# Token-group transposes of a normalized activation by DMA instead of the matmul engine, with group 0's hidden layer moved ahead of its queries

## Chip, cores and metric

The kernel runs on one core of one Trainium2 chip. The metric is the device time in microseconds (us) of one execution; medians of several executions are quoted. Engines are named as in the profile: PE is the matmul engine, PEld its weight loads, DVE the vector engine, ACT the scalar engine, POOL the general one, SP the one that issues the DMA transfers.

Ratios are the mean time of one kernel's fast runs over the mean of the other's fast runs in the same rounds, so they are not quite the ratio of the medians quoted beside them. "Fast" is the state without a disturbance that every run is labelled with.

## The reference

One block for 2048 tokens of width D = 640, all in bf16: `xn` is the layer norm of x, and the result is x plus a linear attention of `xn` plus a feed-forward of `xn`.

```python
def reference(A_x, A_wqkv, A_wo, B_x, B_w1, B_b1, B_w2, B_b2):
    x = A_x
    xn = _layernorm(x)                       # (x - mean) / sqrt(var + 1e-5)
    q, k, v = split(xn @ A_wqkv)             # 32 heads of 20
    pq, pk = phi(q), phi(k)                  # phi(t) = where(t > 0, t + 1, exp(t)) + 1e-6
    kv, z = sum_s pk v^T, sum_s pk           # per head
    attention = (pq kv) / (pq z + 1e-6) @ A_wo
    feed_forward = gelu(xn @ B_w1 + B_b1) @ B_w2 + B_b2      # hidden width 1536
    return x + attention + feed_forward
```
(Shortened: the reshapes are left out.)

## The kernel before

The 2048 tokens are 16 tiles of 128, in 4 groups of 512. `xn` has the tokens on the partitions. The matmuls need the model dimension there, so every tile of `xn` is also transposed into `xnT`: five 128x128 blocks, each a PE matmul against the identity, then one copy from the accumulator bank to `xnT`.

```python
def emit_T(t, copy, c0=0, c1=NC):            # NC = 5
    n = c1 - c0
    pT = bank(BF16)[:, 0 : n * P].rearrange("p (c n) -> p c n", c=n)
    for c in range(n):
        nc.tensor.transpose(pT[:, c, :], xn[:, t, (c0 + c) * P : (c0 + c + 1) * P], identity[:])
    copy(out=xnT[:, c0:c1, t * P : (t + 1) * P], in_=pT)
```

Each group runs K (4 tiles), Q (5 blocks of 5 matmuls), and h (the hidden layer, 12 blocks of 5 matmuls). While a group's h runs on PE, DVE prepares the next group (statistics, 1/sqrt by Newton steps, normalization), and the transposes of the next group are put between the last blocks of h.

```python
for g in range(NG):
    t0, t1 = g * TPG, (g + 1) * TPG
    if g > 0:
        for i in range(TPG):
            emit_K(t0 + i)
    for m in range(NC):
        emit_Q(g, m)
    for j in range(NJ):                       # NJ = 12
        emit_h(g, j)
        # ... cut: sums of pk, masks, late work of the last group ...
        if g == NG - 1:
            continue
        if j < TPG:
            emit_stats(t1 + j)
        if j == TPG:
            emit_rstd_vector(t1, t1 + TPG)    # 13 small DVE operations
        if TPG <= j < 2 * TPG:
            emit_norm(t1 + j - TPG)
        if j > 2 * TPG:
            emit_T(t1 + j - 2 * TPG - 1, nc.scalar.copy)
        if j == NJ - 1:
            emit_T(t1 + TPG - 1, nc.scalar.copy)
```

All loads are issued from SP at the start, in this order: x of tiles 0 and 1, K weights, x of tiles 2 and 3, K weights, Q weights, x of group 1, w1, b1, x of groups 2 and 3, b2, wv, wo, w2.

## Time and profile before

| | before |
|---|---|
| time, median | 213.5 us (213.2 to 214.2, 16 runs) |
| span of the profiled run | 211.9 us |
| PE busy | 98% |
| DVE, ACT busy | 53%, 39% |
| share of PE in the chain that ended last | 95% |

The chain is the work that decided the end: it is followed back from the last instruction, at each step to what released it. These are lines of the profile's page for the kernel before: the span, the busy time of each engine (share of the span, number of instructions), and, from the part on the chain that ended last, the shares of the engines.

```profile
span 211.9 us, 3417 instructions
PE 207.4 (98%) x1393; PEld 119.8 (57%) x1393; DVE 112.2 (53%) x265; ACT 82.8 (39%) x134; POOL 13.3 (6%) x41
...
PE 95%; DMA 3%; SPq 1%; DVE 0%; issue 0%
```

The page is to be read together: PE is nearly always busy, and the chain of work that decides the end is PE's own queue. Shortening work of DVE or ACT buys nothing here. Taking an instruction away from PE buys its time, as long as nothing makes PE wait instead.

What five transposes cost is seen in the chain in order of time, here around the end of group 0's h and the start of group 1's K (start in us, length in us, what, number of instructions). L377 is h, L253 the transposes, L285 is K.

```profile
27.93 2.37 PE bank L377 x11
30.30 0.28 PE bank L253 x5
30.59 1.08 PE bank L377 x5
31.66 0.28 PE bank L253 x5
31.94 1.08 PE bank L377 x5
33.02 0.56 PE bank L253 x10
33.58 1.08 PE bank L285 x5
```

Four sets of five take 1.12 us per group. The groups of instructions say something else for the same matmuls (busy time, then mean ns of one, then idle time before them):

```profile
L253 PE MATMUL bank<-identity,xn 128*128 128x128 bf16 x70 | 5.7, 219 | 0.0
L254 ACT COPY xnT<-bank 128x640 bf16<-128x640 bf16 x13 | 8.6, 690 | 0.5 <-PE bank L253 0.5
```

A single transpose is on record with 219 ns, but the records of a set overlap: five of them take 0.28 us of the chain, 56 ns each. The chain is the view to cost a PE instruction from.

### The profile page before, as it was taken

The page shows a single profiled execution, that of the slowest core. Times are in us where ns is not written, and L with a number is a line of the kernel's source. Part 1 is how long each engine was busy: PE and PEld are TensorE (multiplying, and loading weights), DVE is VectorE, ACT ScalarE, POOL GpSimd, SP SyncE. Part 2 cuts the span into 40 slices and gives each one's busy share as a digit, 9 for nine tenths or more (in the row PEclk, how much of TensorE's full clock was granted, in tenths as well). Part 3 has the DMA queues.
Part 4 walks back from the last instruction along what each step waited for, and adds up shares of the span by engine and source line. Part 5 has one row for each costly group of instructions (what it writes and reads, how often), then busy time and mean ns, then how long its engine had stood idle before and what let it go on. Part 6 is the DMA issues. An engine that isn't in the chain of part 4 may idle for free.

```text
span 211.9 us, 3417 instructions
## 1 busy us (share of the span) xinstructions
PE 207.4 (98%) x1393; PEld 119.8 (57%) x1393; DVE 112.2 (53%) x265; ACT 82.8 (39%) x134; POOL 13.3 (6%) x41
## 2 busy tenths in 40 slices
PE   8999999999999999999999999999999999999993
PEld 2454455544554445544445657677777777777752
DVE  3779950998969995698980021773221121121111
ACT  3576769686786868767441221220000000000000
POOL 1000000000000007000019500000000000000000
PEclk9999999999999999999999999999999999999998
DMA  6999970000000000000049968001101100000111
GB/s 200 348 382 331 361 270 1 5 0 0 0 3 0 0 2 3 0 0 0 3 91 200 195 202 318 10 0 62 34 31 51 45 31 31 31 34 31 59 37 31
DMA packets 13278, 18.17 MB, mean 86 GB/s; under 512 B 2432, under 2 KB 11344, under 8 KB 13264
## 3 DMA queue, kind: packets, MB, share of 16 engines
q1 hardware_dynamic: 13264, 17.97, 27.1%
q8 instruction: 11, 0.18, 0.4%
q14 instruction: 3, 0.02, 0.0%
HBM read 12.72 MB, written 5.24 MB: 85 GB/s over the span
## 4 chain that ended last, share of the span: by engine, by line
PE 95%; DMA 3%; SPq 1%; DVE 0%; issue 0%
PE bank L553 25%; PE bank L377 25%; PE bank L561 10%; PE bank L368 10%; PE bank L470 8%; PE bank L285 8%; DMA wqk<-in_A_wqkv_dram 3%; PE bank L479 2%; PE bank L295 2%; PE bank L253 2%; PE bank L521 1%; PE bank L572 1%; PE bank L339 1%; SPq L127 0%; PE bank L576 0%; PE bank L531 0%
## 5 line engine op out<-in xcount | busy, mean ns | idle before, releaser
L553 PE MATMUL bank<-w,hT 128*128 128x320 bf16 (+2 forms) x384 | 57.3, 299 | 0.0
L377 PE MATMUL bank<-xnT,w 128*128 128x512 bf16 x240 | 53.8, 379 | 0.0
L553 PEld LDWEIGHTS <-hT 128*128 128x128 bf16 x384 | 36.9, 98 | 15.6 <-issue 0.5
L565 DVE TENSOR_TENSOR late<-bank,x_all 128x320 bf16<-128x320 f32 (+2 forms) x32 | 15.7, 492 | 52.2 <-PE bank L561 52.2
L377 PEld LDWEIGHTS <-w 128*128 128x128 bf16 x240 | 23.1, 98 | 26.9 <-issue 0.4
L381 ACT ACTIVATE hT<-bank,b1col 128x512 bf16<-128x512 f32 x48 | 32.6, 687 | 14.0 <-PE bank L377 13.2
L269 ACT ACTIVATE e<-bank 128x512 bf16<-128x512 f32 x40 | 23.0, 596 | 11.7 <-PE bank L368 7.1
L561 PE MATMUL bank<-late,pqT 128*128 128x320 bf16 (+2 forms) x160 | 26.5, 299 | 0.0
L368 PE MATMUL bank<-xnT,wqk 128*128 128x512 bf16 x100 | 22.2, 379 | 0.0
L285 PE MATMUL bank<-wqk,xnT 128*128 128x512 bf16 x80 | 20.4, 379 | 0.1
L561 PEld LDWEIGHTS <-pqT 128*128 128x128 bf16 x160 | 15.5, 98 | 6.3
L270 DVE TENSOR_SCALAR e<-e 128x512 bf16<-128x512 bf16 x40 | 11.4, 285 | 13.6 <-ACT e L269 13.6
L470 PE MATMUL bank<-pk,xn 128*128 128x512 bf16 x80 | 18.1, 379 | 0.0
L368 PEld LDWEIGHTS <-wqk 128*128 128x128 bf16 x100 | 9.6, 98 | 10.9
L206 DVE BATCH_NORM_STATS2 stats<-x_all 128x6 f32<-128x320 bf16 x32 | 13.7, 466 | 3.3 <-DMA x_all<-in_A_x_dram 3.3
L273 DVE SCALAR_TENSOR_TENSOR pk<-bank,e 128x512 bf16<-128x512 f32 x20 | 13.8, 692 | 1.0
L273 DVE SCALAR_TENSOR_TENSOR pqT<-bank,e 128x512 bf16<-128x512 f32 x20 | 13.8, 692 | 0.7
L489 DVE TENSOR_TENSOR pqT<-pqT,xnT 128x2048 bf16<-128x2048 bf16 x5 | 6.0, 1215 | 15.4 <-DMA xnT<-rec_rows 15.4
L470 PEld LDWEIGHTS <-xn 128*128 128x128 bf16 x80 | 7.7, 98 | 8.5
L359 DVE TENSOR_TENSOR zacc<-zacc,pk 128x640 f32<-128x640 f32 x13 | 10.8, 829 | 0.4
L285 PEld LDWEIGHTS <-xnT 128*128 128x128 bf16 x80 | 7.1, 98 | 5.6 <-issue 0.4
L471 ACT CAST GT<-bank 128x512 bf16<-128x512 f32 x5 | 2.9, 587 | 16.9 <-PE bank L470 16.9
(68 smaller groups left out, 124.6 us busy)
## 6 DMA issues: line engine op xcount, KB each, us to landing
w<-in_B_w_dram SPq DMA_DIRECT2D x2, 1920.0 KB, 10.0
rec_rows<-recT SPq DMA_DIRECT2D x4, 640.0 KB, 8.3
xnT<-rec_rows SPq DMA_DIRECT2D x5, 512.0 KB, 6.7
out_dram<-late SPq DMA_DIRECT2D x15, 160.0 KB, 1.8
x_all<-in_A_x_dram SPq DMA_DIRECT2D x3, 640.0 KB, 9.3
wqk<-in_A_wqkv_dram SPq DMA_DIRECT2D x1, 800.0 KB
wv<-in_A_wqkv_dram SPq DMA_DIRECT2D x1, 800.0 KB
woA<-in_A_wo_dram SPq DMA_DIRECT2D x5, 160.0 KB, 7.5
```

The source lines that it names most:

```text
L206: nc.vector.bn_stats(out=st[:, half, :], in_=x_all[:, t, half * HALF : (half + 1) * HALF])
L269: nc.scalar.activation(out=e[:], in_=ps[:], func=ACT.Exp)
L270: nc.vector.tensor_scalar(out=e[:], in0=e[:], scalar1=1.0, scalar2=1e-6, op0=ALU.min, op1=ALU.add)
L273: nc.vector.scalar_tensor_tensor(out=dst, in0=shaped(ps), scalar=0.0, in1=shaped(e), op0=ALU.max, op1=ALU.add)
L285: nc.tensor.matmul(K_ps[t][:], lhsT=xnT[:, k, t * P : (t + 1) * P], rhs=wqk[:, k, D : D + TOK], start=(k == 0), stop=(k == NC - 1),)
L368: nc.tensor.matmul(ps[:], lhsT=wqk[:, k, m * P : (m + 1) * P], rhs=xnT[:, k, gs], start=(k == 0), stop=(k == NC - 1),)
L377: nc.tensor.matmul(ps[:], lhsT=w1[:, k, j * P : (j + 1) * P], rhs=xnT[:, k, g * TOK : (g + 1) * TOK], start=(k == 0), stop=(k == NC - 1),)
L381: nc.scalar.activation(out=hT[g][:, j, :], in_=ps[:], func=ACT.Gelu_apprx_tanh, bias=b1col[:, j : j + 1], scale=1.0)
L470: nc.tensor.matmul(ps[:], lhsT=w, rhs=pk[:, t, 0:TOK], start=(t == 0), stop=(t == NT - 1))
L553: nc.tensor.matmul(ps, lhsT=hT[g][:, j, i * P : (i + 1) * P], rhs=w2[:, j, ns], start=(j == 0), stop=False)
L561: nc.tensor.matmul(ps, lhsT=pqT[:, c, t * P : (t + 1) * P], rhs=KVW[:, c, ns], start=False, stop=(c == NC - 1),)
L565: nc.vector.tensor_tensor(out=osb[:, ns], in0=ps, in1=x_all[:, t, ns], op=ALU.add)
```

## The change

Its intent: groups 1 to 3 are transposed by the DMA engines. A group's `xn` is stored to a DRAM buffer, and five transposing DMA transfers (512 rows by 128 columns each) bring it back as `xnT`. That path has a long latency, so the rest of the change makes room for it: group 0's h moves ahead of its Q, w1 is loaded before the Q weights, 1/sqrt goes to POOL, and the loads that are needed late are issued only after group 2's transposes.

```diff
+    def emit_T_dma(g):
+        rows = xn_rows[g]
+        nc.sync.dma_start(
+            out=rows[:].rearrange("(i p) d -> p i d", p=P), in_=xn[:, g * TPG : (g + 1) * TPG, :]
+        )
+        for c in range(NC):
+            nc.sync.dma_start(
+                out=xnT[:, c, g * TOK : (g + 1) * TOK], in_=rows[:, c * P : (c + 1) * P], transpose=True
+            )
 ...
-    def emit_rstd_vector(t0, t1):             # 13 Newton operations on DVE
+    def emit_rstd_pool(t0, t1):
+        r = rstd[:, t0:t1]
+        nc.gpsimd.tensor_scalar(out=r, in0=mv[:, t0:t1, 1], scalar1=EPS, scalar2=None, op0=ALU.add)
+        nc.gpsimd.tensor_tensor(out=r, in0=r, in1=neg_half[:, 0 : t1 - t0], op=ALU.pow)
 ...
     load_wk(3, NC)
+    load_x(4, 8)
+    # b1, then w1 in two halves
     # Q weights
-    # x of group 1, w1, b1
     load_x(8, 12)
-    load_x(12, 16)                            # and b2, wv, wo, w2
+    def load_late(): ...                      # the same five loads
 ...
+    # group 0's K; statistics, rstd and norms of group 1
+    emit_T_dma(1)
+    for t in range(2, TPG + 1):
+        emit_K0phi(t)                         # the rest of group 0's phi(K)
+    # statistics, rstd and norms of group 2
+    emit_T_dma(2)
+    load_late()
     for g in range(NG):
+        if g == 0:
+            for j in range(NJ):
+                emit_h(g, j)
         # K if g > 0, Q, then h if g > 0
+            if g == 1 and j == 0:
+                # statistics, rstd and norms of group 3
+                emit_T_dma(3)
-            if j > 2 * TPG:
-                emit_T(t1 + j - 2 * TPG - 1, nc.scalar.copy)
-            if j == NJ - 1:
-                emit_T(t1 + TPG - 1, nc.scalar.copy)
```
(One of the sums of pk on DVE also moves to the next group's h, and the other sums of groups 1 and 2 and the masks on POOL are issued earlier within it; a fourth buffer for exp is added, and group 0's K banks are held longer.)

More of the change, by code (lines that the diff above doesn't have):

```diff
@@ L12 @@
 F32 = mybir.dt.float32
-I32 = mybir.dt.int32
 @with_exitstack
@@ L70 @@
     small = ctx.enter_context(tc.tile_pool(name="small", bufs=4))
-    etmp = ctx.enter_context(tc.tile_pool(name="etmp", bufs=3))
+    etmp = ctx.enter_context(tc.tile_pool(name="etmp", bufs=4))
     psum = ctx.enter_context(tc.tile_pool(name="psum", bufs=1, space=bass.MemoryType.PSUM))
@@ L82 @@
     rec_rows = dram.tile([H * DH, S], BF16, name="rec_rows")
+    xn_rows = {g: dram.tile([TOK, D], BF16, name=f"xn_rows{g}") for g in range(1, NG)}
     zsum = GT[:, NC - 1, :]
@@ L98 @@
     Z3t = consts.tile([P, NC, H], BF16, name="Z3t")
-    newton = consts.tile([P, 2, TPG], F32, name="newton")
+    neg_half = consts.tile([P, TPG], F32, name="neg_half")
     eps_t = consts.tile([P, 1], F32, name="eps_t")
@@ L135, with load_late @@
     load_wk(3, NC)
+    load_x(4, 8)
+    nc.sync.dma_start(out=b1_bf[:], in_=B_b1.rearrange("(j p) -> p j", p=P))
+    nc.sync.dma_start(out=w1[:, :, 0 : F // 2], in_=w1_v[:, :, 0 : F // 2])
+    nc.sync.dma_start(out=w1[:, :, F // 2 : F], in_=w1_v[:, :, F // 2 : F])
     nc.sync.dma_start(out=wqk[:, :, 0:D], in_=wqkv_v[:, :, 0:D])
-    load_x(4, 8)
-    nc.sync.dma_start(out=w1[:], in_=w1_v)
-    nc.sync.dma_start(out=b1_bf[:], in_=B_b1.rearrange("(j p) -> p j", p=P))
     load_x(8, 12)
-    load_x(12, 16)
-    nc.sync.dma_start(out=b2b[:], in_=B_b2.unsqueeze(0).to_broadcast((P, D)))
-    nc.sync.dma_start(out=wv[:], in_=wqkv_v[:, :, 2 * D : 3 * D])
-    for m in range(NC):
-        nc.sync.dma_start(out=woA[:, m, :], in_=A_wo[e_lo[m] : e_lo[m] + P, :])
-    nc.sync.dma_start(out=w2[:], in_=w2_v)
+    def load_late():
+        load_x(12, 16)
+        nc.sync.dma_start(out=b2b[:], in_=B_b2.unsqueeze(0).to_broadcast((P, D)))
+        nc.sync.dma_start(out=wv[:], in_=wqkv_v[:, :, 2 * D : 3 * D])
+        for m in range(NC):
+            nc.sync.dma_start(out=woA[:, m, :], in_=A_wo[e_lo[m] : e_lo[m] + P, :])
+        nc.sync.dma_start(out=w2[:], in_=w2_v)
     nc.vector.memset(warm, 0.0)
     nc.vector.memset(eps_t[:], EPS)
+    nc.vector.memset(neg_half[:], -0.5)
     make_identity(nc, identity)
@@ L217, in emit_rstd @@
         nc.scalar.activation(out=r, in_=r, func=ACT.Exp, scale=-0.5)
-    def emit_rstd_vector(t0, t1):
-        n = t1 - t0
-        y = rstd[:, t0:t1]
-        v, a = newton[:, 0, 0:n], newton[:, 1, 0:n]
-        nc.vector.tensor_scalar(out=v, in0=mv[:, t0:t1, 1], scalar1=EPS, scalar2=None, op0=ALU.add)
-        nc.vector.tensor_scalar(
-            out=a.bitcast(I32), in0=v.bitcast(I32), scalar1=1, scalar2=None,
-            op0=ALU.logical_shift_right,
-        )
-        nc.vector.tensor_scalar(
-            out=y.bitcast(I32), in0=a.bitcast(I32), scalar1=-1.0, scalar2=float(0x5F3759DF),
-            op0=ALU.mult, op1=ALU.add,
-        )
-        nc.vector.tensor_scalar(out=v, in0=v, scalar1=-0.5, scalar2=None, op0=ALU.mult)
-        for _ in range(3):
-            nc.vector.tensor_tensor(out=a, in0=v, in1=y, op=ALU.mult)
-            nc.vector.tensor_tensor(out=a, in0=a, in1=y, op=ALU.mult)
-            nc.vector.scalar_tensor_tensor(
-                out=y, in0=a, scalar=1.5, in1=y, op0=ALU.add, op1=ALU.mult
-            )
+    def emit_rstd_pool(t0, t1):
+        r = rstd[:, t0:t1]
+        nc.gpsimd.tensor_scalar(out=r, in0=mv[:, t0:t1, 1], scalar1=EPS, scalar2=None, op0=ALU.add)
+        nc.gpsimd.tensor_tensor(out=r, in0=r, in1=neg_half[:, 0 : t1 - t0], op=ALU.pow)
     def emit_norm(t, c0=0, c1=NC):
@@ L265, in emit_T_first, with phi_exp, phi_rest @@
             nc.scalar.copy(out=xnT[:, c0:c1, t * P : (t + 1) * P], in_=pT)
-    def phi(dst, ps, shaped):
+    def phi_exp(ps):
         e = etmp.tile([P, TOK], BF16, name="e")
         nc.scalar.activation(out=e[:], in_=ps[:], func=ACT.Exp)
+        return e
+    def phi_rest(dst, ps, e, shaped):
         nc.vector.tensor_scalar(
@@ L275, in phi @@
         )
+    def phi(dst, ps, shaped):
+        phi_rest(dst, ps, phi_exp(ps), shaped)
     rest_ps = {}
@@ L282, in emit_Ka @@
         if k0 == 0:
-            K_ps[t] = bank()
+            K_ps[t] = bank(hold=t < TPG)
         for k in range(k0, k1):
@@ L408, with emit_K0phi @@
     emit_norm(3)
+    e_of = {}
+    def emit_K0phi(t):
+        if t < TPG:
+            phi_rest(pk[:, t, 0:TOK], K_ps.pop(t), e_of[t], lambda a: a[:])
+        else:
+            phi_rest(
+                pk[:, 0:TPG, TOK:D], rest_ps[0], e_of[t],
+                lambda a: a[:].rearrange("p (t n) -> p t n", t=TPG),
+            )
     emit_Ka(1, 2, NC)
     emit_Kb(1)
-    emit_Kphi(0)
+    e_of[0] = phi_exp(K_ps[0])
+    emit_K0phi(0)
     emit_Ka(2, 0, 2)
@@ L415 @@
     emit_Kb(2)
-    emit_Kphi(1)
-    emit_Kphi(2)
-    emit_K(3)
+    e_of[1] = phi_exp(K_ps[1])
+    e_of[2] = phi_exp(K_ps[2])
+    emit_Ka(3)
+    emit_Kb(3)
+    e_of[3] = phi_exp(K_ps[3])
+    e_of[TPG] = phi_exp(rest_ps[0])
+    emit_stats(4)
+    nc.vector.tensor_copy(out=b1col[:], in_=b1_bf[:])
+    for t in range(5, 8):
+        emit_stats(t)
+    emit_rstd_pool(4, 8)
+    emit_K0phi(1)
+    for t in range(4, 8):
+        emit_norm(t)
+    emit_T_dma(1)
+    for t in range(2, TPG + 1):
+        emit_K0phi(t)
+    for t in range(8, 12):
+        emit_stats(t)
+    emit_rstd_pool(8, 12)
+    for t in range(8, 12):
+        emit_norm(t)
+    emit_T_dma(2)
+    load_late()
     for g in range(NG):
         t0, t1 = g * TPG, (g + 1) * TPG
+        if g == 0:
+            for j in range(NJ):
+                emit_h(g, j)
+                if j == 7:
+                    release()
+            nc.scalar.preload_act_table_set("natural_log_exp_and_others")
         if g > 0:
-            nc.scalar.preload_act_table_set("natural_log_exp_and_others")
+            if g > 1:
+                nc.scalar.preload_act_table_set("natural_log_exp_and_others")
             for i in range(TPG):
@@ L426 @@
             emit_Q(g, m)
-            if g == 0 and m == 2:
-                nc.vector.tensor_copy(out=b1col[:], in_=b1_bf[:])
         if g == NG - 1:
             hT.append(early.tile([P, NJ, TOK], BF16, name="hT3", tag="early"))
-        for j in range(NJ):
+        for j in range(NJ if g > 0 else 0):
             emit_h(g, j)
-            if g == 1 and j == 2 * TPG:
+            if g == 1 and j == 0:
+                for t in range(3 * TPG, NT):
+                    emit_stats(t)
+                emit_rstd_pool(3 * TPG, NT)
+                for t in range(3 * TPG, NT):
+                    emit_norm(t)
+                emit_T_dma(3)
                 emit_zacc(0)
+            if g == 2 and j == 0:
+                gate(hT[g][:, 0, 0:1])
+                emit_masks()
                 emit_zacc(1)
-            if g == 2 and j == 2 * TPG:
-                gate(xn[:, NT - 1, 0:1])
-                emit_masks()
                 emit_zacc(2)
@@ L449 @@
                     emit_xb(t)
-            if g == NG - 1:
-                continue
-            if j < TPG:
-                emit_stats(t1 + j)
-            if j == TPG:
-                emit_rstd_vector(t1, t1 + TPG)
-            if TPG <= j < 2 * TPG:
-                emit_norm(t1 + j - TPG)
-            if j > 2 * TPG:
-                emit_T(t1 + j - 2 * TPG - 1, nc.scalar.copy)
-            if j == NJ - 1:
-                emit_T(t1 + TPG - 1, nc.scalar.copy)
     grest = [None]
```

## The prediction

> **What bounds the kernel now.** The profile's page has the matmul engine (PE) busy 98% of a 211.9 us span; the chain of waits that ended last is 95% PE; the granted clock is 0.997. So a change pays only by taking instructions off PE, and costs only by making PE wait. DVE (53%) and ACT (39%) have room.
>
> **What the change removes from PE.** 12 of the 14 five-fold transposes of line 253 (60 small matmuls). In the chain in order of time, hidden-layer blocks start at 30.59 and 31.94 us with 1.08 us of matmul: 0.27 us per five transposes. The chain gives line 253 1.9%, 4.0 us for 14 sets, which agrees. 12 x 0.275 = 3.3 us, all critical. Also gone: 12 ACT copies of 0.69 us and 39 DVE Newton steps of 0.16 us, off the critical path, worth nothing directly.
>
> **What it adds.** Per group one store of xn to DRAM and five DMA transposes 512x128, plus two small POOL operations. To hide their latency, group 0's hidden layer goes ahead of its Q, and w1 is loaded before the Q weights.
>
> **Does PE have to wait?**
> (a) w1. K of group 0 ends at 14.0 us; then w1's first half is needed. Ahead of it are 2.13 MB, the 2-byte-element load of b1, and its own 0.98 MB. By the GB/s of 1 us windows, 3.1 MB had moved at 11.1 us before; b1 shows as a dip at 15 to 17 us worth 0.9 us; landing trails by about 1.5 us (wqk at 8.4). Estimate: 13.5 us, nearly no margin. I allow 0.3 us.
> (b) The first Gelu waits for five exponentials and a table load (1.28 us) and ends near 16.9 us; three free banks carry PE to 17.3. Fits.
> (c) xnT of group 1. Its K is due at 14.0 + 12x1.08 + 5x1.08 = 32.4 us. DVE finishes the norms of tiles 4 to 7 near 19.5 us (statistics 4.1, norms 1.7, phi 1.0, POOL 1). The store (0.66 MB) lands near 23.5. Five issues of about 0.5 us, then about 2 us: ready near 28 us, slack 4 us. The Trainium skill, "DMA: Bandwidth & Descriptors", section "Latency and other measured facts", gives 261 GB/s for such transposes, 2.5 us a group; but "VectorE: DVE Perf Modes", "The three transpose paths", gives 1309 ns for one 128x128. Were those serial, 20 would take 26 us and PE would stop for some 17 us. No trace here shows a DMA transpose yet. I think the first is nearer.
> (d) Groups 2 and 3 (due near 56 and 80 us) have over 15 us of slack; the late loads behind group 2's transposes are needed from 45 us on (x). DVE in h of group 1 carries about 9 of 13 us. Fits.
>
> **Prediction.** 213.5 - 3.3 + 0.3 (w1) + about 0.2 (weighted small waits) = 210.7 us; range 209.4 to 214.5. Faster by over 2%: 0.04; within 2%: 0.84; slower: 0.12.
>
> **What would show it right or wrong.** PE instructions down by 60 (from 1393); PE busy down by about 3.3 us, to near 204; line 253's share down to 2 sets; no idle PE from 14 to 130 us beyond 1 us in the 40 slices; DMA transposes of group 1 landed before 32 us; chain over 93% PE.
>
> **What would make it wrong.** Transposes over about 8 us a group (PE idle at 32 us, the DMA of xnT in the chain); the b1 load holding up w1 (PE idle at 14 us); x of tiles 12 to 15 landing late, so that DVE holds up banks near 45 us; POOL's power operation taking several us.

## More of the kernel before

The profile's list of PE's waits (who, for what, us in total, times, longest) has a single line, at the start of the kernel; PE waits for ACT nowhere:

```profile
PE bank L192 <- DVE hT L149: 1.1, 1, 1.1
```

## The result, and the profile after

| | before | after |
|---|---|---|
| time, median | 213.49 us (213.18 to 214.24, 16 runs) | 210.02 us (209.52 to 210.41, 8 runs) |
| ratio of fast runs | | 0.9835, 95% interval 0.982 to 0.985 |
| span of the profiled run | 211.9 us | 208.4 us |
| PE instructions | 1393 | 1333 |

The changed kernel is 1.65% faster; a second series of it, on another occasion (e12 below), gave 0.9862 (0.9834 to 0.9890). The same parts of its page:

```profile
span 208.4 us, 3281 instructions
PE 203.5 (98%) x1333; PEld 116.4 (56%) x1333; DVE 106.7 (51%) x227; ACT 75.7 (36%) x122; POOL 18.4 (9%) x47
...
PE 95%; DMA 3%; SPq 1%; issue 0%; DVE 0%
```

PE has exactly 60 instructions fewer and still sets the end: PE 98% busy, 95% of the chain. Everything that PE waited for in the whole run is in the list of its waits (who, for what, us in total, times, longest), and all of it lies in the first 9 us:

```profile
PE bank L196 <- DVE hT L152: 1.1, 1, 1.1
PE bank L259 <- DVE xn L230: 0.6, 1, 0.6
PE bank L289 <- DMA wqk<-in_A_wqkv_dram: 0.3, 1, 0.3
```

In the chain, the starts of K (L289 now) of groups 1, 2 and 3, with h and Q (L381 and L372) of group 0 ahead of the first:

```profile
14.27 12.99 PE bank L381 x60
27.26 5.39 PE bank L372 x25
32.66 1.08 PE bank L289 x5
...
56.44 1.08 PE bank L289 x5
...
80.21 1.08 PE bank L289 x5
```

The same two later starts in the chain of the kernel before:

```profile
58.48 1.08 PE bank L285 x5
...
83.37 1.08 PE bank L285 x5
```

K of group 1 starts 0.92 us earlier than before (33.58 - 32.66; the start of the kernel had cost 0.15 us more in this run), K of group 2 2.04 us and K of group 3 3.16 us earlier: 1.12 us per group, which is the four sets of transposes of that group and nothing else. After group 3 PE gains no more: the output addition that ends the chain starts 3.19 us earlier (first the kernel before, then the changed one):

```profile
208.75 0.29 DVE late L565
```

```profile
205.56 0.29 DVE late L601
```

The spans differ by 3.5 us. The other 0.3 us lies behind that addition, in the last stores and the end of the program: 3.2 us from it to the end of the span in the kernel before and in e1 below, 2.8 to 2.9 us in every run with DMA transposes, e2 (the old order) among them. What shortens this end is not shown.

The new path can be followed in SP's issues in order of time (start, length, engine, line, operation):

```profile
19.62 0.39 SPq L246 DMA_DIRECT2D xn_rows<-xn  x1
22.88 6.44 SPq L250 DMA_TRANSPOSE xnT<-xn_rows  x5
29.48 0.47 SPq L246 DMA_DIRECT2D xn_rows<-xn  x1
32.81 6.35 SPq L250 DMA_TRANSPOSE xnT<-xn_rows  x5
39.20 1.33 SPq L127 DMA_DIRECT2D x_all<-in_A_x_dram  x1
```

Group 1's store is issued at 19.62 us and the transposes may start when it has landed, 3.3 us later. Then the five transposes are issued one after the other, each taking SP about 1.25 us. One lands 2.7 us (median) after its issue began, so the last, issued at 28.1, landed at about 30.8 us (this one's landing is not on record; the estimate uses the median). PE began group 1's K at 32.5. The slack, counted to there, was about 1.7 us. It was really somewhat larger: where PE has to wait (e2, e3 and e8 below) it takes `xnT` block by block, and only the fifth matmul of K, 0.86 us after the first, needs the last block, so about 2.6 us.

POOL's two operations, three times each, were no obstacle:

```profile
L226 POOL TENSOR_TENSOR rstd<-rstd,neg_half 128x4 f32<-128x4 f32 x3 | 3.1, 1041 | 0.2
...
L225 POOL TENSOR_SCALAR rstd<-mv 128x4 f32<-128x4 f32 x3 | 0.7, 230 | 45.2 <-DVE mv L212 45.2
```

### The profile page after: what moved, and what is told of

Its sections match the earlier page's. It is cut to its first block, busy times and chain, and to the rows that moved or that the text cites. A ratio compares the mean times of both kernels' runs of the same rounds, so it can differ in the third digit from the quotient of the medians.

```text
span 208.4 us, 3281 instructions
## 1 busy us (share of the span) xinstructions
PE 203.5 (98%) x1333; PEld 116.4 (56%) x1333; DVE 106.7 (51%) x227; ACT 75.7 (36%) x122; POOL 18.4 (9%) x47
## 4 chain that ended last, share of the span: by engine, by line
PE 95%; DMA 3%; SPq 1%; issue 0%; DVE 0%
PE bank L589 25%; PE bank L381 25%; PE bank L597 10%; PE bank L372 10%; PE bank L506 8%; PE bank L289 8%; DMA wqk<-in_A_wqkv_dram 3%; PE bank L515 2%; PE bank L299 2%; PE bank L557 1%; PE bank L608 1%; PE bank L343 1%; SPq L127 0%; PE bank L240 0%; PE bank L612 0%; PE bank L567 0%
## 5 line engine op out<-in xcount | busy, mean ns | idle before, releaser
L381 PE MATMUL bank<-xnT,w 128*128 128x512 bf16 x240 | 52.8, 379 | 0.0
L381 PEld LDWEIGHTS <-w 128*128 128x128 bf16 x240 | 23.2, 98 | 28.1 <-issue 0.4
L385 ACT ACTIVATE hT<-bank,b1col 128x512 bf16<-128x512 f32 x48 | 32.5, 687 | 15.7 <-PE bank L381 15.5
L267 ACT ACTIVATE e<-bank 128x512 bf16<-128x512 f32 x40 | 23.0, 596 | 13.8 <-PE bank L372 7.7
L372 PE MATMUL bank<-xnT,wqk 128*128 128x512 bf16 x100 | 22.2, 379 | 0.0
L289 PE MATMUL bank<-wqk,xnT 128*128 128x512 bf16 x80 | 20.4, 379 | 0.3 <-DMA wqk<-in_A_wqkv_dram 0.3
L271 DVE TENSOR_SCALAR e<-e 128x512 bf16<-128x512 bf16 x40 | 11.4, 285 | 13.4 <-ACT e L267 13.3
L372 PEld LDWEIGHTS <-wqk 128*128 128x128 bf16 x100 | 9.6, 98 | 11.1
L274 DVE SCALAR_TENSOR_TENSOR pk<-bank,e 128x512 bf16<-128x512 f32 x20 | 13.8, 692 | 1.0
L274 DVE SCALAR_TENSOR_TENSOR pqT<-bank,e 128x512 bf16<-128x512 f32 x20 | 13.8, 692 | 0.7
L289 PEld LDWEIGHTS <-xnT 128*128 128x128 bf16 x80 | 7.2, 98 | 6.5 <-issue 0.5
```

Of the source, the lines that this page charges most:

```text
L267: nc.scalar.activation(out=e[:], in_=ps[:], func=ACT.Exp)
L271: nc.vector.tensor_scalar(out=e[:], in0=e[:], scalar1=1.0, scalar2=1e-6, op0=ALU.min, op1=ALU.add)
L274: nc.vector.scalar_tensor_tensor(out=dst, in0=shaped(ps), scalar=0.0, in1=shaped(e), op0=ALU.max, op1=ALU.add)
L289: nc.tensor.matmul(K_ps[t][:], lhsT=xnT[:, k, t * P : (t + 1) * P], rhs=wqk[:, k, D : D + TOK], start=(k == 0), stop=(k == NC - 1),)
L372: nc.tensor.matmul(ps[:], lhsT=wqk[:, k, m * P : (m + 1) * P], rhs=xnT[:, k, gs], start=(k == 0), stop=(k == NC - 1),)
L381: nc.tensor.matmul(ps[:], lhsT=w1[:, k, j * P : (j + 1) * P], rhs=xnT[:, k, g * TOK : (g + 1) * TOK], start=(k == 0), stop=(k == NC - 1),)
```

## The experiments

The theory: the whole gain is the PE time of 60 transposes; everything else in the change only keeps PE from waiting, and is worth nothing by itself. The rivals: the new order or the relief of ACT and DVE gave part of the gain; or the transposes would have fitted in without the rest.

### e1_pe_transposes: everything but the DMA transposes

```diff
-    emit_T_dma(1)        # and (2), (3)
+            # in h of groups 0, 1 and 2, as in the kernel before:
+            if j > 2 * TPG:
+                emit_T(t1 + j - 2 * TPG - 1, nc.scalar.copy)
+            if j == NJ - 1:
+                emit_T(t1 + TPG - 1, nc.scalar.copy)
```

> The changed kernel with the 60 transposes of groups 1 to 3 back on PE (and their ACT copies), everything else of the change kept (w1 loaded first, hidden layer of group 0 first, POOL rstd, late loads, zacc moved). Theory: the whole gain is PE time of the transposes, 12 sets of 0.275 us, so 210.0 + 3.3 = 213.3 us, no gain left over before (213.5), PE instructions 1393. Rival: the reordering itself, or the relief of ACT (8.3 us of copies) and DVE, gave part of it; reordering alone would then leave 210.5 to 212.

Measured: 213.64 us (213.25 to 214.18, 6 runs), ratio to before 0.9999 (0.9977 to 1.0021). The order, POOL's 1/sqrt and the later loads are worth nothing that can be measured when the transposes are on PE. That part of the rival falls. The relief of ACT is not separated by this run, since the 12 copies came back with the transposes; against it speaks that PE waited for ACT nowhere in the kernel before, and the count in the chain above. (In this profile 14 matmul records are missing; the weight loads are the 1393 that were expected.)

### e9_group1_on_pe: one group's transposes back on PE

```diff
-    emit_T_dma(1)
+            # in h of group 0 only: emit_T as above
```

> The changed kernel with group 1's 20 transposes back on PE, groups 2 and 3 by DMA. Theory: one third of the gain returns, 210.0 + 1.1 = 211.1 us, linear in the number of transposes on PE. Rival (gain from the relief of DMA, DVE or order): no such step, or a different one.

Measured: 210.88 us (210.79 to 211.12, 5 runs), ratio 0.9870 (0.9848 to 0.9891). By the times alone this is not clear, since the unaltered changed kernel gave 0.9835 and, on another occasion, 0.9862 (e12 below). The chain is clear. Two of its starts of K (groups 1 and 2) are:

```profile
33.22 1.08 PE bank L289 x5
...
57.00 1.08 PE bank L289 x5
```

Group 0's h began at 13.73 us in this run, so from there to K of group 1 it is 19.49 us against 18.39 (32.66 - 14.27) in the changed kernel: 1.10 us more, for 20 transposes. From K of group 1 to K of group 2, whose transposes are by DMA, it is 23.78 us in both (57.00 - 33.22 and 56.44 - 32.66); it was 24.90 before (58.48 - 33.58). The gain is counted out in transposes.

### e2_dma_alone: only the DMA transposes

The kernel before with one part of the change (the definition of `emit_T_dma` and its buffer, as above, are left out).

```diff
-            if j > 2 * TPG:
-                emit_T(t1 + j - 2 * TPG - 1, nc.scalar.copy)
-            if j == NJ - 1:
-                emit_T(t1 + TPG - 1, nc.scalar.copy)
+            if j == 2 * TPG:
+                emit_T_dma(g + 1)
```

> The kernel before with one part of the change alone: transposes by DMA in place of PE, no reordering, no POOL rstd, loads in the old order. Theory: the norms of group 1 end at about 29.7 us; store about 3.3, five issues of 1.25, 2.7 to land: ready near 41 us, due near 32.4, so PE waits about 9 us there, and again for groups 2 and 3: about 213.5 - 3.3 + 3 x 8 or 9 = 235 us, PE idle about 25 us in three places before L285. Rival (the transposes are quick enough to fit without the reordering): 211 to 214 us.

Measured: 241.13 us (239.93 to 241.75, 4 runs), ratio 1.1276 (1.1240 to 1.1311), slower by more than expected. From the list of waits, and from the stretches of 2 us around group 1's K (the length of the stretch, busy us of PE, PEld, DVE, ACT, POOL with instruction counts, then the granted clock of PE, which is the share of its full clock that it was allowed, the DMA share, GB/s):

```profile
PE bank L297 <- DMA xnT<-xn_rows: 19.3, 14, 4.9
```

```profile
32.00:34.00 2.00, 1.20 (x6) 0.35 (x4) 0.00 (x0) 1.43 (x3) 0.00 (x0) 1.00 0.63 227
...
36.00:38.00 2.00, 0.00 (x0) 0.00 (x0) 0.00 (x0) 0.00 (x0) 0.00 (x0) 0.50 0.29 66
...
46.00:48.00 2.00, 2.00 (x10) 1.12 (x9) 0.67 (x2) 0.60 (x1) 0.00 (x0) 0.50 0.00 0
...
50.00:52.00 2.00, 1.95 (x14) 1.06 (x14) 1.60 (x4) 1.14 (x3) 0.00 (x0) 1.00 0.03 8
```

PE ended group 0's h at 33.2 us and could start K's fifth matmul, the first that needs the last fifth of `xnT`, only at 43.4. Without a wait it would have started 0.86 us after h, so it was 9.3 us late; for groups 2 and 3 it was 7.1 and 7.4 us. That is 23.7 us, close to the 25 expected, less 3.3 for the transposes. (The list's 19.3 us leave out the matmuls that PE did between the waits.) The measured loss is 27.6, so about 7 us were not foreseen, and the third number from the right in the lines points to where they are: after the wait the granted clock is 0.50 while PE is fully busy (46 to 48 us), and back at 1.00 only around 49 us. From that fifth matmul to Q, K takes 7.5, 7.7 and 5.9 us in the three groups, where 4.74 us are enough after a wait at full clock (e10 below): 6.9 us in all. The rest of the change is thus what makes the DMA transposes pay. That the clock is the cause of the slow K is at this point only a reading; e10 tests it, on e3.

### e3_late_loads_first: the late loads issued at the start again

```diff
     load_x(8, 12)
+    load_late()
 ...
     emit_T_dma(2)
-    load_late()
```

> The changed kernel with the late loads (x of tiles 12 to 15, b2, wv, wo, w2) issued at the start as before. Theory: these 4.8 MB sit on the queue ahead of group 1's store until about 31 us, so the store lands near 32 us, the transposes near 40 us, and PE waits 6 to 9 us before group 1's K: 216 to 219 us. Rival: the order of the late loads does not matter, since the store needs only 0.66 MB: 210 to 211 us.

Measured: 221.46 us (220.82 to 222.88, 4 runs), ratio 1.0384 (1.0347 to 1.0422). The rival falls: group 1's store, issued at 22.4 us, landed at 33.9 behind the bulk, 11.5 us after its issue instead of 3.3. Again the loss, 11.4 us by the medians, is about 2 us larger than the wait, from 32.4 to 41.9 us.

### e10_fill_the_wait: the same, with useless matmuls in the wait

The result is the right one; the 43 matmuls go into a bank that nobody reads.

```diff
 # e3_late_loads_first, and
+            if g == 1:
+                emit_warm(43)                 # 43 matmuls 128x512 of no use
             for i in range(TPG):
                 emit_K(t0 + i)
```

> The kernel of e3_late_loads_first (221.5 us) with 43 matmuls of no use put before group 1's K, where PE had waited from 32.4 to 41.9 us: at 0.216 us each they fill 9.3 us. Theory: of the 11.4 us that e3 lost, 9.4 was the wait and 2.0 the half clock that the profile shows after it; the useless work keeps the clock at 1.0, so 210.0 + 9.4 = 219.4 us, faster with more work. Rival: the 2 us are a backlog of DVE, ACT or the queue after the wait, and the useless work changes nothing: 221.5 us or more.

Measured: 220.19 us (219.17 to 221.07, 6 runs), ratio 1.0290 (1.0262 to 1.0319), against 1.0384 for e3. The difference of the ratios is 2.0 us, that of the medians 1.3: the kernel with 43 matmuls more is faster. The clock of the profiled run is 1.0 (0.977 in e3). The chain shows the place. First e3, from the landing of the last transpose to group 1's Q (L373; L290 and L300 are K):

```profile
39.11 2.75 DMA xnT<-xn_rows
...
41.90 0.61 PE bank L290
...
43.05 2.13 PE bank L290 x5
...
48.35 0.22 PE bank L373
```

Then the same in e10:

```profile
41.03 2.93 DMA xnT<-xn_rows
...
44.01 0.39 PE bank L290
...
44.68 1.08 PE bank L290 x5
...
48.75 1.29 PE bank L373 x6
```

The transposes landed 2.1 us later in e10's profiled run, which the theory did not foresee and which may be why the time is 0.8 us above the 219.4 expected. But the same K takes 6.45 us in e3 (41.90 to 48.35) and 4.74 us in e10 (44.01 to 48.75), and five matmuls take 2.13 us instead of 1.08. So the surcharge on a wait is the clock: 1.7 us here. The Trainium skill, "TensorE: Matmul & The Clock Gate", section "What's actually happening", describes half clock after an idle window of about 3.4 us, watched in windows that run free of the kernel. The halved matmuls here agree with it, and e2's trace shows the windows: its clock changes at 35.29, 48.94, 72.84, 83.08, 106.97 and 113.80 us, and the steps between are 4, 7, 3, 7 and 2 times 3.41 us. But a window need not be idle throughout: the clock fell 2.1 us after PE's last matmul in e2 (33.2 to 35.3) and 2.7 us after it in e3 (32.4 to 35.2).

### e8_half_transposes: does the issue cost go with the size?

```diff
-            # one transfer of 512 rows
+            for h in range(2):                # two of 256 rows
+                nc.sync.dma_start(
+                    out=xnT[:, c, g * TOK + h * TOK // 2 : g * TOK + (h + 1) * TOK // 2],
+                    in_=rows[h * TOK // 2 : (h + 1) * TOK // 2, c * P : (c + 1) * P], transpose=True,
+                )
```

> The changed kernel with each DMA transpose cut into two of 256 rows (30 instead of 15). If the queue takes a fixed 1.25 us for each transpose, a group takes 12.5 us, the ninth lands near 36 us and PE waits about 3.5 us before group 1's K: 213.5 us (groups 2 and 3 have the slack). If the time goes with the size (0.63 us each), the group takes 6.3 us as now: 210.0 us.

Measured: 213.48 us (212.45 to 214.60, 6 runs), ratio 0.9985 (0.9950 to 1.0020). SP's issues of group 1:

```profile
23.06 12.76 SPq L251 DMA_TRANSPOSE xnT<-xn_rows  x10
```

Ten half transposes take twice the time of five whole ones: 1.28 us each, whether 256 or 512 rows. The cost is one of issuing, not of bytes, between these two sizes. That eats the slack and more, and the whole gain of the change is gone. The runs also fall into two heaps: 212.45, 212.55 and 212.89 us with a clock of 1.0, and 214.07, 214.54 and 214.60 us with 0.992. In the profiled run (one of the slower ones) PE waits 0.4 and then 2.2 us, with one matmul between, and the half clock lasts from 35.8 to 39.2 us, 3.4 us in which PE is busy nearly throughout: the price is again some 1.7 us, and the means of the heaps are 1.8 us apart. That a wait of the same length sometimes costs the half clock and sometimes does not would fit the skill's window that runs free of the kernel, but the faster heap has no profile, so its waits are not known.

### e4_transposes_later: group 1's store later in the program

```diff
-    emit_T_dma(1)
     for t in range(2, TPG + 1):
         emit_K0phi(t)
+    emit_T_dma(1)
```

> The changed kernel with group 1's store and transposes emitted three phi steps later on DVE's order (only DVE's order of waiting matters: the store is issued by the queue once the norms are done, and norms stay ahead of the phi steps). Theory A (the store is released by the norms' own semaphore count, 19.6 us): no change, 210.0 us. Theory B (the store waits for the DVE count at its place in the program, after the phi steps, at 22.4 us): transposes land 2.8 us later, near 33.6, PE waits about 1.1 us at 32.5: 211.1 us.

Measured: 210.06 us (209.96 to 210.32, 4 runs), ratio 0.9835 (0.9815 to 0.9856): no difference, theory A. The store is issued at 19.14 us, when the norms are done and before the first of the three phi steps that now precede it in the program has ended. It waits for the norms, not for its neighbours, so this experiment did not use up any slack.

### e5_newton_on_dve: 1/sqrt on DVE again

```diff
-    nc.gpsimd.tensor_scalar(... op0=ALU.add); nc.gpsimd.tensor_tensor(... op=ALU.pow)
+    # the 13 Newton operations of the kernel before, on nc.vector
```

> The changed kernel with rstd by the Newton steps on DVE again (13 operations of about 0.2 us in a row) in place of two POOL operations. Theory: norms of group 1 end about 2.0 us later (21.6 instead of 19.6), the transposes land near 32.8 us, due at 32.5: PE waits 0.2 to 0.6 us, 210.2 to 210.7 us. Rival: the slack is larger than 2 us, 210.0 us; or DVE falls behind elsewhere, over 211 us.

Measured: 209.73 us (209.65 to 210.38, 4 runs), ratio 0.9825 (0.9802 to 0.9847); PE never waits for the transposes. The expected 2.0 us of delay were 1.4 (the store is issued at 21.01 us instead of 19.62). The last transpose, issued at 29.5, landed by the estimate above at about 32.2 us, and K started at 32.9, with its fifth matmul, which needs that block, at about 33.7. So some 1.5 us of slack were left, and unused slack has no price. Moving 1/sqrt to POOL is not needed for this time; it only keeps a margin.

### e6_w1_whole: w1 in one load

```diff
-    nc.sync.dma_start(out=w1[:, :, 0 : F // 2], in_=w1_v[:, :, 0 : F // 2])
-    nc.sync.dma_start(out=w1[:, :, F // 2 : F], in_=w1_v[:, :, F // 2 : F])
+    nc.sync.dma_start(out=w1[:], in_=w1_v)
```

> The changed kernel with w1 in one load. Theory: the whole w1 lands near 16.0 us (1.2 MB more than 3.1 MB at 370 GB/s after the first half's estimated 13.5), so PE waits 1.5 to 2.5 us before the first hidden-layer block at 14.1, 211.5 to 212.5 us. If the half load landed much before 14.1, the wait is smaller.

Measured: 212.26 us (211.35 to 215.32, 6 runs, one of them slow), ratio of the fast runs 0.9941 (0.9906 to 0.9976). In the profile:

```profile
PE bank L380 <- DMA w<-in_B_w_dram: 1.2, 1, 1.2
```

The split of w1 is worth it: without it PE waits at the first block of h, and the time scatters. K of group 0 ended at 13.8 us in this run and w1 was there at 15.0. Two of the six runs, 213.92 and 215.32 us (the one labelled slow), have a granted clock of 0.992, as the slower heap of e8 has; no profile of them was kept. When the first half of the split w1 lands is on record in three runs with the same loads: at 12.9 us in e1, 13.5 in e9 and 14.3 in e5, where it stands in the chain (L398 is h) and PE's first weight load of h waited 0.3 us for it:

```profile
3.72 10.61 DMA w<-in_B_w_dram
...
14.37 5.78 PE bank L398 x26
```

So the split has little to spare.

### e11_head_order and e12_after_again: an attempt at a faster version

PE's only idle time left is in the first 9 us, so e11 reorders the loads there.

```diff
-    load_x(0, 2)
+    load_x(0, 1)
     load_wk(0, 3)
-    load_x(2, 4)
+    load_x(1, 2)
     load_wk(3, NC)
+    load_x(2, 4)
 ...
-    emit_Ka(1, 0, 2)
+    emit_Ka(1)
+    emit_Kb(1)
     emit_T(2, nc.vector.tensor_copy)
     # ... and Ka(1, 2, NC), Kb(1) no longer after emit_norm(3)
```

> An attempt at a faster version: the changed kernel with x of tile 0 loaded alone first, x of tile 1 after the first part of the K weights, x of tiles 2 and 3 after all K weights, and tile 2's transposes after all of K of tile 1. PE's only idle time left in the changed kernel is in the first 9 us (0.6 before the first transposes, 0.3 before the fourth matmul of K). Theory: the first transposes start 0.4 us earlier and K's weights land 0.9 us earlier, so K of group 0 ends near 13.6 instead of 14.1: 209.5 us. Rival: tiles 2 and 3 land later and PE waits for their norms as much as it gained: 210.0 to 210.5 us.

> The changed kernel unaltered, to compare with e11_head_order on the same chip: 210.0 us, ratio to the kernel before 0.9835.

Measured on the same chip: e11 211.21 us (211.14 to 211.49, 5 runs), ratio 0.9885 (0.9863 to 0.9906); the changed kernel 210.90 us (209.61 to 211.42, 6 runs), ratio 0.9862 (0.9834 to 0.9890). The attempt failed: it is not faster, and by the ratios not clearly slower either. Group 0's h begins at 15.13 us in e11's profile and at 13.71 in e12's. PE's waits in e11 tell why:

```profile
PE bank L260 <- DVE xn L231: 0.6, 1, 0.6
PE bank L290 <- DVE xnT L242: 0.6, 1, 0.6
```

The first transposes did not start earlier (6.95 us against 6.28), although x of tile 0 was loaded alone, and PE then waits for tile 2. Why the smaller first load did not bring tile 0 sooner was not pursued.

No experiment gave a version faster than the changed kernel.

## Why the prediction was right

- **The bound and the size of the gain.** Right. 12 x 0.275 = 3.3 us was predicted for PE. The chains show 1.12 us per group from group to group, and 3.19 us at the output addition that ends it; 0.3 us more at the end of the program were not predicted and are not explained. e1 shows that the order, the loads and POOL's 1/sqrt gained nothing: with the transposes on PE the whole rest of the change measures 0.9999 (0.9977 to 1.0021). The other marks held too: PE busy 203.5 us (near 204 was predicted), 95% of the chain (over 93%).
- **The waits.** The allowance for waits, 0.3 us for w1 and 0.2 us for the rest, was not used in the profiled run: the profile of the changed kernel has no wait of PE after 9 us. Without that allowance the sum is 210.2, against a measured median of 210.02 us; with it the prediction was 0.7 us too high. The second series of the same kernel (e12) gave 210.90, so the scatter between series is of that size too, and the two can't be told apart by the time alone.
- **(a) w1.** Right. The landing of the first half was estimated at 13.5 us with "nearly no margin"; where it is on record it is 12.9, 13.5 and 14.3 us (under e6). PE did not wait for it in the profile of the changed kernel, and in e5's the weight load waited 0.3 us, just the allowance.
- **(c) group 1's transposes.** Right that they land in time, but the margin was wrong: the forecast was ready at 28, slack 4 us; the trace gives about 30.8 and, counted the same way, 1.7 us. The store was on time (22.9 against 23.5). The step that failed is "five issues of about 0.5 us, then about 2 us": an issue takes 1.25 us and the landing 2.7. That the result held all the same was partly luck: the slack happened to be larger than this error, and e8 shows the gain lost when it is not. Five transfers of 131,072 bytes from first issue to last landing take about 7.9 us, 83 GB/s, by the estimate of 30.8. The Trainium skill's 261 GB/s ("DMA: Bandwidth & Descriptors", section "Latency and other measured facts"), which the page gives for a source with a non-contiguous middle dimension, was not reached by a kernel that issues them in pieces of this size, and its 1309 ns for one 128x128 block ("VectorE: DVE Perf Modes", section "The three transpose paths") did not add up serially over the 20 blocks either: that would have been 26 us, an estimate from the page's figure.
- **(d) the later groups.** Right: PE never waited for them.
- **What would have made it wrong.** "Transposes over about 8 us a group" was near: store, issues and landing took 11.2 us, 7.9 of it the transposes. e8 shows what would have followed: PE waits of 2.6 us in all, and the gain gone.
- **Left out of the prediction.** A wait of PE was priced at its length. e10 shows that a long one cost about 1.7 us more, for the clock.

## What to carry to other kernels

When PE is 98% busy and its own chain sets the end, an instruction moved off PE pays what it occupies in the chain (56 ns here, not the 219 ns on its record), and the rest of such a change is only worth the waits that it avoids: alone, the DMA transposes made this kernel 13% slower, and the reordering alone did nothing. Before moving work to DMA, write down when the data must be there, and cost the way in issues and landings rather than in bytes; keep bulk loads that are needed late out of the queue ahead of it. If PE must wait for two microseconds or more, add the slow clock after it to the price: some 1.7 us in e3 and e8, 6.9 us for the three waits of e2.

## What the Trainium skill lacked or had wrong

- "DMA: Bandwidth & Descriptors" lacks a time, for Trainium2, of what a DMA transpose from DRAM costs its issuing engine (it has a count of cycles for small tiles of "previous generations"): 1.25 us for 512 rows by 128 columns and 1.24 us for 256 rows by 128 (medians), so a fixed cost for an instruction at these sizes (a plain load or store took SP about 0.4 us when the queue was free). Five in a row landed at about 83 GB/s, where its section "Latency and other measured facts" has 261 GB/s.
- "Advanced Engine Details and Errata", section "X-Bar Transpose (TRN2)", says "TRN2 transpose DMAs are as fast as regular DMAs". Here a plain store of 0.66 MB landed 3.3 us after its issue, and the five transposes of the same data took about 7.9 us, 5.2 of them from the first issue to the last.
- "VectorE: DVE Perf Modes", section "The three transpose paths", gives single-block figures (390 ns for PE, 1309 ns for DMA) from which a stream cannot be costed: in the chain a PE transpose took 56 ns, and four blocks in one DMA transpose landed 2.7 us after the issue began.
- "TensorE: Matmul & The Clock Gate" advises against PE idling for more than about 3 us. Here waits of 0.4 and 2.2 us (e8) already cost the clock, and some 1.7 us with it, and in e2 2.1 us of idle time did. Its description of fixed windows is borne out by e2's steps of 3.41 us; that they run free of the kernel's start fits the two heaps of e8's times, but is not shown.
- No page has the time of the power operation on POOL: 1.04 us for 128x4.
